# First batch of a two-stage attention and ReGLU kernel: idle matmuls at the start, a changed stage order, a changed split of casts

## Chip, cores and metric

The kernel runs on one core of a Trainium2 chip. The metric is device time in microseconds (us), the median of several executions. Before the change: 700.3 us, median of 5 runs from 699.91 to 702.34 (702.34, 700.5, 700.3, 700.12, 699.91).

## What is computed

Inputs in float32: `x` (4 batches, 12416 rows, 128 columns), 32 `inducing` rows of 128, and three feed-forward weights. Cut to what matters:

```python
h   = softmax(scale * I @ x.T) @ x        # per batch: 32 rows h, over all 12416 rows of x
a   = softmax(scale * x @ h.T) @ h        # per batch: every row of x against those 32
out = (relu(a @ w_gate) * (a @ w_val)) @ w_out      # 128 -> 1536 -> 128
```

Nothing of a batch's second line can start before its `h` is complete, since `h` sums over all rows of that batch.

## The kernel before

**Two kinds of work.** For each batch a first phase computes `h`; after it a long loop computes attention and feed-forward for the rows, 512 at a time and in pairs. The first phase of batches 1 to 3 is spread through the loop of the batch ahead of it. The first phase of batch 0 has nothing to hide behind: the loop can't start before it has ended. The change is in that phase alone.

**First phase of batch 0.** The 97 tiles of 128 rows come in 16 parts (`sizes`, lines 73 to 77): nine of 8 tiles (j0, j1, j2, j4 to j9), six of 4 (j10 to j15), and as j3 a single tile. SP (SyncE) issues their loads in this order, then those of the weights (L251 to L253). No edit touches a load. Each part passes through four stages, each of which issues on fixed engines:

- `cast` (L271): float32 to fp16 into `x16`. The first `h` tiles go to POOL (GpSimd, L278), the others to ACT (ScalarE, L280). For 8 tiles the split is 4 and 4, for 4 tiles 2 and 2. The single tile goes to DVE (VectorE, L275).
- `turn` (L264): PE (TensorE) transposes the part tile by tile into a PSUM bank (L268); DVE copies the result to `xT` (L269).
- `score` (L282): PE multiplies each tile with the inducing rows (L287); ACT takes the exponential into `p1` (L289).
- `sums` (L291): PE adds up the softmax denominators (L297 for the large parts, L306 for the small) and the 32 rows `hT_ps` (L309).

In addition `reduce` (L311) folds the large parts' denominators on DVE, L295 adds them in on PE, and `idle` (L260) issues matmuls of 512 columns whose results nobody reads. The PSUM tiles of `turn` and `score` take turns in three banks of tag "g"; `p1` has four buffers.

**The order.** The engines run what they are given in program order. That order is written by a small planner (lines 319 to 339): each stage of each part gets a due time, computed from the number of tiles landed and a few constants, and the stages are emitted in order of due time. From the part that begins at tile 64 (`late`, j9) on, 1.4 is added, and there three idle matmuls precede the turn. A due time isn't a wait; it only decides which stage is ahead of which in each engine's queue.

**After it** (lines 340 to 354): POOL casts the weights (L341), three idle matmuls, `finish_h` (DVE, L145 and L147), then the first matmuls with `h` (L178 and L159), DVE's copy `hgv` (L349), and the loop (L924 on), where ACT's relu (L998) and DVE's product (L1010) are the main work.

Of the kernel before, what the change touches and what calls it, by code (L numbers as in the profile page):

```python
# [11 lines left out]
FP16 = mybir.dt.float16  # L12
# [6 lines left out]
def kernel(  # L19
# [16 lines left out]
    nc = tc.nc  # L36
# [3 lines left out]
    P = 128  # L40
    assert C == P and M == 32 and N % P == 0 and DFF % P == 0
    NT = N // P
    BLK = 512
# [15 lines left out]
    def bank(tag, name, shape=None, dtype=FP32):  # L59
        return psum.tile(  # L60
            shape or [P, BLK], dtype, tag=tag, bufs={"g": 3, "v": 2, "o": 1}[tag], name=name
        )

    def st(shape, dtype, tag, bufs, name=None):
        return sb.tile(shape, dtype, tag=tag, bufs=bufs, name=name or tag)
# [32 lines left out]
    eye16 = constp.tile([P, P], FP16, name="eye16")  # L98
# [8 lines left out]
    nc.vector.memset(ones16, 1.0)  # L107
    minus1 = constp.tile([P, 4 * TPB], FP32, name="minus1")
    nc.gpsimd.memset(minus1, -1.0)

    ind16 = constp.tile([M, C], FP16, name="ind16")
    nc.vector.tensor_copy(out=ind16, in_=ind32)
# [114 lines left out]
    z1a, idle_ps = z1a_ps[:, 0 : 8 * M], z1a_ps[:, BLK : 2 * BLK]  # L227
# [28 lines left out]
    n_parts = len(parts)  # L256
# [3 lines left out]
    def idle(ps, n, rhs):  # L260
        for _ in range(n):
            nc.tensor.matmul(ps[:, 0 : rhs.shape[-1]], eye16, rhs, start=True, stop=True)
# [8 lines left out]
    def cast(j):  # L271
        t0, t1 = parts[j]
        x32, dst, n = x32s[j], x16[:, t0:t1, :], t1 - t0
        if n == 1:
            nc.vector.tensor_copy(out=dst, in_=x32)  # L275
            return
        h = n // 2 if n != 4 or j == n_parts - 1 else 2
        nc.gpsimd.tensor_copy(out=dst[:, 0:h, :], in_=x32[:, 0:h, :])  # L278
        if h < n:
            nc.scalar.copy(out=dst[:, h:, :], in_=x32[:, h:, :])  # L280
# [38 lines left out]
    stages = []  # L319
    landed = 0  # L320
    late = [j for j in range(n_parts) if parts[j][0] >= 64 and parts[j][1] < NT][0]
    for j, (t0, t1) in enumerate(parts):
        n = t1 - t0
        landed += n
        at = 0.16 * landed + (1.4 if j >= late else 0)
        stages.append((at - (0.6 if j == n_parts - 1 else 0), 0, j, cast))
        at += 0.1 + 0.065 * n
        if j == late:
            idles = lambda j: idle(idle_ps, 3, xT[0][:, 0:4, :].rearrange("p t c -> p (t c)"))
            stages.append((at, 1, j, idles))  # L330
        stages.append((at, 2, j, turn))
        if j == n_parts - 1:
            stages.append((at + 0.3, 3, j, reduce))
        at += 0.05 * n + 0.5 + 0.068 * n + (0.6 if n > 4 else 0.15)
        stages.append((at, 3, j, score))
        at += 0.025 * n + 0.6 + 0.026 * n + (0.6 if n > 4 else 0.3)
        stages.append((at, 4, j, sums))
    for _, _, j, f in sorted(stages, key=lambda e: e[0:3]):
        f(j)
# [160 lines left out]
    def plan_phase1(b):  # L500
# [9 lines left out]
        for q in range(NCH):  # L510
# [17 lines left out]
            at = at0 + 14 * q if q < NQ else at0 + 7  # L528
            post[at + 3].append(load)
            post[at + 11].append(cast)  # L530
            post[at + 15].append(transp)

# [383 lines left out]
    idle_ps = bank("o", "idle_ps")  # L916
# [7 lines left out]
    at = 0  # L924
# [3 lines left out]
    while True:  # L928
# [24 lines left out]
        if jobs:  # L953
            j = jobs[0]
# [89 lines left out]
```

The softmax here doesn't subtract the row's maximum and nothing guards it: scores larger than these inputs give would overflow.

## Time and profile before

| | |
|---|---|
| profiled execution | 700.05 us |
| its span on the core | 698.3 us (1.75 us lie around it) |
| median of 5 runs | 700.3 us |
| busy share of the span, PE / DVE / ACT / POOL | 91% / 97% / 96% / 53% |
| DMA, share of the 16 engines' time taken by the main queue (q1) | 47.9% |
| first product of the loop that lasts (L1010, 1024 columns) | starts at 29.72 us |

How to read it: DVE and ACT are busy for nearly the whole span, but that is an average. Their busy time in the first 25 us is 11.01 and 12.96 us; the loop starts only after that. A row of the timeline has its start, its length, the engine, the line, the operation and how many instructions were merged (x8); a bracket tells how long the engine was idle before it, and who ended that. The chain of waits has start, length, engine, tile and line.

### The profile page before, as it was taken

To read this page: it belongs to the slowest core of one execution; us is meant where nothing else is said; L and a number is where in the kernel's file an instruction comes from. 1 tells how busy PE (TensorE), PEld (TensorE's weight loads), DVE (VectorE), ACT (ScalarE), POOL (GpSimd) and SP (SyncE) were. 2 spreads that over 40 slices of the span, in tenths; PEclk is the share of its full clock that TensorE was granted. 3 is DMA by queue.
4 is the path that set the end of the run, shared out by engine and by line. 5 is a ranking of instruction groups with operands and counts; after the bars stand their busy time and mean duration, and the time that the engine had idled before them with its cause. 6 is when DMAs were issued, how large, how long until landed. Compare 5 with 4: busy or idle time off the path is not lost.

```text
span 698.3 us, 13986 instructions
## 1 busy us (share of the span) xinstructions
PE 632.4 (91%) x4571; PEld 181.3 (26%) x4571; DVE 676.5 (97%) x617; ACT 672.7 (96%) x1381; POOL 370.7 (53%) x680
## 2 busy tenths in 40 slices
PE   6999998999999999999999999998999898888897
PEld 5422222222222222222222222222222222222224
DVE  4699999999999999999999999999999999999997
ACT  4799999999999999999999999999999999999996
POOL 4618647645276565665257474873534543534443
PEclk9999999999999999999999999999999999999999
DMA  9666776541666848513176776533223231231222
GB/s 346 222 127 177 168 171 168 116 84 62 137 174 161 209 135 167 132 58 92 50 193 166 205 185 146 131 95 69 68 72 85 57 92 56 80 85 53 76 56 91
DMA packets 142633, 87.57 MB, mean 125 GB/s; under 512 B 117184, under 2 KB 125664, under 8 KB 140256
## 3 DMA queue, kind: packets, MB, share of 16 engines
q1 hardware_dynamic: 142368, 86.60, 47.9%
q8 instruction: 35, 0.57, 0.3%
q14 instruction: 38, 0.31, 0.2%
q10 hardware_dynamic: 192, 0.08, 0.1%
HBM read 27.80 MB, written 25.43 MB: 76 GB/s over the span
## 4 chain that ended last, share of the span: by engine, by line
ACT 40%; PE 26%; issue 18%; DVE 14%; DMA 2%; SPq 0%; POOL 0%; ACTq 0%; DVEq 0%
ACT g L998 29%; DVE gv L1010 13%; PE o_ps L690 10%; PE v_ps L901 8%; ACT oT L696 6%; PE g_ps L901 3%; ACT p2q L194 2%; ACT p1T L549 1%; PE xT_ps L268 1%; PE o_ps L757 1%; DMA gv<-in_x_dram 1%; ACT hgv L169 1%; DMA out_dram<-osb 1%; DVE xT L269 0%; DMA o<-oT 0%
## 5 line engine op out<-in xcount | busy, mean ns | idle before, releaser
L1010 DVE TENSOR_TENSOR gv<-g,v_ps 128x1024 f16<-128x1024 f16 (+1 forms) x578 | 657.2, 1209 | 3.4 <-ACT g L998 1.0
L998 ACT ACTIVATE g<-g_ps 128x512 f16<-128x512 f32 (+1 forms) x1168 | 603.5, 618 | 6.6 <-PE g_ps L901 1.9
L690 PE MATMUL o_ps<-gv,wo 128*128 128x512 f16 x1128 | 352.4, 384 | 46.0 <-ACT oT L696 45.8
L707 POOL TENSOR_SCALAR osb<-o,z2i 128x128 f32<-128x128 f16 x380 | 164.5, 447 | 229.9 <-DMA o<-oT 219.0
L901 PE MATMUL g_ps<-p,hgv 32*128 32x512 f16 x1152 | 282.5, 379 | 0.8 <-ACT g L998 0.5
L901 PE MATMUL v_ps<-p,hgv 32*128 32x512 f16 x1152 | 223.6, 384 | 5.5 <-DVE gv L1010 4.3
L901 PEld LDWEIGHTS <-hgv 32*128 32x128 f16 x2400 | 66.7, 91 | 267.2 <-issue 262.9
L690 PEld LDWEIGHTS <-wo 128*128 128x128 f16 x1176 | 80.8, 97 | 212.5 <-issue 198.7
L446 POOL TENSOR_TENSOR z2i<-zt,minus 128x16 f32<-128x16 f32 (+3 forms) x31 | 73.2, 2363 | 0.5
L696 ACT CAST oT<-o_ps 128x512 f16<-128x512 f32 (+1 forms) x98 | 59.3, 605 | 0.1
L439 POOL TENSOR_TENSOR zt<-zt 128x32 f32<-128x32 f32 (+5 forms) x124 | 34.9, 281 | 9.7
L517 POOL CAST x<-x 128x2048 f16<-128x2048 f32 x18 | 34.0, 1890 | 11.2 <-DMA x<-in_x_dram 10.7
L439 POOL TENSOR_TENSOR zt<-p2T 128x256 f32<-128x256 f16 (+3 forms) x31 | 17.4, 561 | 32.0 <-DMA p2T<-p2q 17.2
L269 DVE COPY xT<-xT_ps 128x1024 f16<-128x1024 f16 (+1 forms) x15 | 8.6, 583 | 9.4 <-PE xT_ps L268 8.7
L593 POOL TENSOR_TENSOR zq<-p1g 128x256 f32<-128x256 f16 x18 | 12.0, 668 | 6.9 <-DMA p1g<-p1T 6.9
L278 POOL CAST x<-gv 128x512 f16<-128x512 f32 (+1 forms) x15 | 7.9, 528 | 11.7 <-DMA gv<-in_x_dram 11.6
L194 ACT ACTIVATE p2q<-s_ps 128x512 f16<-128x512 f32 x22 | 13.4, 611 | 0.0
L268 PE MATMUL xT_ps<-eye,x 128*128 128x128 f16 x97 | 10.4, 258 | 2.2 <-POOL x L278 1.3
L595 POOL TENSOR_TENSOR zq<-zq 128x256 f32<-128x256 f32 x15 | 10.9, 725 | 1.2
L289 ACT ACTIVATE p<-s_ps 128x256 f16<-128x256 f32 (+2 forms) x16 | 5.2, 333 | 6.3 <-PE s_ps L287 6.2
L280 ACT CAST x<-gv 128x512 f16<-128x512 f32 (+1 forms) x15 | 7.5, 532 | 3.8 <-DMA gv<-in_x_dram 3.8
L549 ACT ACTIVATE p1T<-s1T_ps 128x512 f16<-128x512 f32 x18 | 11.0, 612 | 0.0
(93 smaller groups left out, 165.6 us busy)
## 6 DMA issues: line engine op xcount, KB each, us to landing
out_dram<-osb SPq DMA_DIRECT2D x95, 256.0 KB, 2.2
x<-in_x_dram SPq DMA_DIRECT2D x18, 1024.0 KB, 5.7
p<-p2q SPq DMA_DIRECT2D x88, 64.0 KB, 2.0
gv<-in_x_dram SPq DMA_DIRECT2D x9, 512.0 KB, 6.7
o<-oT SPq DMA_TRANSPOSE x98, 2.4
gv<-in_x_dram SPq DMA_DIRECT2D x6, 256.0 KB, 8.5
x<-in_moe_w_out_dram SPq DMA_DIRECT2D x1, 768.0 KB, 9.6
x<-in_moe_w_gate_dram SPq DMA_DIRECT2D x1, 512.0 KB, 7.1
```

What stands on the lines that cost most here:

```text
L194: nc.scalar.activation(out=p2q, in_=ps, func=AF.Exp, scale=sm_scale)
L268: nc.tensor.transpose(ps[:, t - t0, :], x16[:, t, :], eye16)
L439: nc.gpsimd.tensor_tensor(out=dst, in0=v[:, :, :, 0:m], in1=v[:, :, :, m : 2 * m], op=ALU.add)
L446: nc.gpsimd.tensor_tensor(out=z2i, in0=v[:, :, :, 0], in1=minus1[:, 0 : n * g].rearrange("p (n g) -> p n g", n=n), op=ALU.pow,)
L517: nc.gpsimd.tensor_copy(out=s["x16"][:, t0:t1, :], in_=s["x32", q])
L549: nc.scalar.activation(out=p1T, in_=ps, func=AF.Exp, scale=sm_scale)
L690: nc.tensor.matmul(c["ps"][:, 0:w], wo[:, i, :], gv(i), start=(i == 0), stop=(i == NFF - 1))
L696: nc.scalar.copy(out=oT[:, 0:w], in_=c["ps"][:, 0:w])
L707: nc.gpsimd.tensor_scalar(out=osb[:, t, :], in0=o16[:, t, :], scalar1=zz, scalar2=zz, op0=ALU.mult, op1=ALU.mult,)
L901: nc.tensor.matmul(ps[:, cols], hgv[:, s * P : (s + 1) * P], p2, start=True, stop=True)
L998: nc.scalar.activation(out=g16[:, k * w : (k + 1) * w], in_=ps[:, 0:w], func=AF.Relu)
L1010: nc.vector.tensor_tensor(out=dst[:, ks, :], in0=g16[:, ks, :], in1=v[:, ks, 0:w], op=ALU.mult)
```

## The change

Four edits. (1) A tile `warm` of zeros is made on POOL, and eight matmuls of 512 columns with it stand first in PE's order; one more stands ahead of the turns of j1 and j2. (2) In the four-tile parts, the last excepted, POOL casts 3 tiles and ACT 1, where it was 2 and 2. (3) The due times of `score` and `sums` have other constants. (4) The last part's `cast` is due 0.3 ahead of its landing, where it was 0.6.

```diff
+    warm = st([P, BLK], FP16, "oT", 4)
+    nc.gpsimd.memset(warm, 0.0)
+    warm_ps = bank("o", "warm_ps")
+    for _ in range(8):
+        nc.tensor.matmul(warm_ps, eye16, warm, start=True, stop=True)
...
-        h = n // 2 if n != 4 or j == n_parts - 1 else 2
+        h = n // 2 if n != 4 or j == n_parts - 1 else 3
...
-        stages.append((at - (0.6 if j == n_parts - 1 else 0), 0, j, cast))
+        stages.append((at - (0.3 if j == n_parts - 1 else 0), 0, j, cast))
...
+        if 0 < j < 3:
+            stages.append((at, 1, j, lambda j: idle(idle_ps, 1, warm)))
         stages.append((at, 2, j, turn))
...
-        at += 0.05 * n + 0.5 + 0.068 * n + (0.6 if n > 4 else 0.15)
+        at += 0.05 * n + 0.5 + 0.068 * n + (0.6 if n != 4 else 0.3)
         stages.append((at, 3, j, score))
-        at += 0.025 * n + 0.6 + 0.026 * n + (0.6 if n > 4 else 0.3)
+        at += 0.025 * n + 0.6 + 0.026 * n + (0.8 + 0.6 if n == 1 else 0.8 if n == 8 else 0.3)
         stages.append((at, 4, j, sums))
```

In the engines' queues this comes to the following. PE: eight idle matmuls ahead of the transpose of the inducing rows, two more later; the score of the single tile j3 moves behind that of j1, its sums behind the turn of j5; the turns of j7 and j8 move ahead of the sums of j4 and j5; small exchanges from j8 on. ACT: the cast of j4 moves ahead of the exponential of j3; five casts are 128 columns wide where they were 256. POOL: one memset ahead of everything that waits for data; five casts are 384 columns wide where they were 256. DVE's and SP's orders stay as they were, and no DMA is added, taken away or moved. The first use of the buffer that `warm` held waits, among other things, for that memset.

## The prediction

> **What bounds the kernel now.** I read three things in this order: the busy time by stage, the chain of waits of the first 36 us, and the timeline there. The stage table (columns: stretch, its length, busy time of PE, weight loads, DVE, ACT, POOL, granted clock, DMA share, GB/s):
>
> ```profile
> 0.00:5.00 5.00, 0.20 (x1) 0.10 (x1) 1.38 (x8) 1.43 (x2) 0.86 (x8) 1.00 0.59 198
> 10.00:15.00 5.00, 4.80 (x89) 4.06 (x86) 2.24 (x4) 3.34 (x8) 2.45 (x4) 1.00 1.03 406
> 30.00:35.00 5.00, 4.89 (x33) 1.67 (x33) 5.00 (x5) 5.00 (x12) 4.08 (x5) 1.00 0.42 174
> ```
>
> From 30 us on ACT and DVE are full; nothing in the change touches that loop. Before it, PE and DMA are full and ACT is not. So the change is worth what it moves the loop's start, and the loop carries that to the end if nothing in it hangs on a fixed time. The chain says what the start hangs on:
>
> ```profile
> 12.86 0.05 issue
> 12.91 0.61 PE xT_ps L268 x4
> 13.52 0.21 PE s_ps L287 x8
> 13.73 0.21 PE z1a_ps L297
> 13.94 0.21 PE hT_ps L309 x8
> 14.15 0.56 PE xT_ps L268 x8
> 14.71 0.19 PE s_ps L287 x8
> 14.91 0.12 PE z1a_ps L297
> ...
> 24.58 0.10 PE hT_ps L309 x4
> 24.68 0.66 PE z1a_ps L262 x3
> 25.34 0.03 issue
> 25.36 0.40 PE s_ps L178 x4
> ```
>
> PE almost without a break. The same sum over 256 columns (L297) costs 0.21 at 13.73 and 0.12 at 14.91: PE's rate nearly doubles at about 14.1, though the granted clock reads 1.00 in every stage. The timeline agrees:
>
> ```profile
> 6.79 1.04 PE L268 MATMUL xT_ps<-eye,x 128*128 128x128 f16 x8 [0.20 <-POOL x L278]
> 15.06 0.61 PE L268 MATMUL xT_ps<-eye,x 128*128 128x128 f16 x8
> 15.35 1.10 POOL L278 CAST x<-gv 128x512 f16<-128x512 f32 x2 [0.66 <-DMA gv<-in_x_dram]
> 17.94 0.81 PE L262 MATMUL z1a_ps<-xT,eye 128*128 128x512 f16 x3
> 18.16 1.53 ACT L280 CAST x<-gv 128x512 f16<-128x512 f32 x4
> 20.55 0.40 POOL L278 CAST x<-gv 128x256 f16<-128x256 f32 x1 [0.27 <-DMA gv<-in_x_dram]
> ```
>
> Part j9 has landed at 15.35, when POOL casts its half, but ACT casts the other half at 18.16, 2.8 later: ACT's queue has the exponential of j8 ahead of it, and that waits for PE. The last part lands at 20.55.
>
> **Rates.** From the chain, for a part of 8 tiles at the fast rate: transposes 0.46, scores 0.21, sums 0.12 + 0.19 = 0.31; together 0.98. At the slow rate: transposes 0.86 (8 x 0.107; 1.04 less some 0.18 of tail that the merged row at 15.06 also has), scores 0.21, sums 0.42; together 1.49. Parts land every 1.28 (POOL's casts at 10.24, 11.52, 12.79, 14.08). So a slow PE falls 0.2 behind on each part and a fast one gains 0.3. Other steps: DVE starts 0.2 after the last transpose, occupies 0.61 and can be read 0.74 after its start (16.67 to 17.41); an exponential starts 0.46 after the first score (17.42 to 17.88), frees ACT after 0.28 and can be read after 0.4; an ACT cast of 512 columns occupies 0.52, the next transposes go 0.67 after its start.
>
> **The idle matmuls at the start.** POOL's memset of 512 fp16 columns has no row; it lies between its memset of 128 columns (0.20) and its cast of 512 (0.61). I take 0.6, since nothing on POOL waits until 4.89; it ends by 1.95. Eight slow matmuls of 512 columns: three fast ones take 0.66 in the chain at 24.68, so 0.22 each, slow 1.9 times that, 0.42; 8 x 0.42 = 3.4, to about 5.4. Queued behind them is the transpose of the inducing rows, which ran at 4.29; its copy is then there at 5.85 and first needed by the scores of j0 at 7.5. The turn of j0 waits for its cast until 5.55 anyway; it loses at most 0.1, which the wait for the landing of j1 (6.1) covers.
>
> **When PE becomes fast.** No row shows it for the new order. In the trace the rate rose at 14.1: that is 3.7 after PE's work became gapless (10.44), or 8.55 after it became regular (5.55). Put on a start at 1.9 this gives 5.6 and 10.45; the far bound is no gain, 14.1 as now. I take 7.4, towards the nearer bound, since PE then has work without a break from 1.9 to 7.8. [...]
>
> **The walk.** With release at 7.4, and the new queues: turn of j2 ends 9.38, scores of j1 follow, their exponential runs at 9.84, the cast of j4 at 10.12 (10.44 before). From here each part goes: cast on ACT, transposes, sums, scores, exponential. Scores of j4 begin 12.68, of j5 13.64, of j6 14.61, of j7 15.57 (trace of before: 13.31, 14.55, 15.51, 16.47); the cast of j8 is at 14.38, 0.3 behind its landing, where it was 1.2 behind. The turn of j8 ends 15.27, DVE's copy starts 15.47, scores 16.21, exponential 16.67; ACT is free for j9 at 16.95, not 18.16. That is 1.2. The same walk through the old order with release at 14.1 puts this cast at 18.07 and the end of the sums at 24.6, where the trace has 18.16 and 24.68, so I trust it to about 0.1.
>
> **The tail.** From the cast of j9 to the last sum took 24.68 - 18.16 = 6.52. The 3:1 split makes five ACT casts 128 columns wide: 512 take 0.61 and 256 take 0.40, so 128 take about 0.29 and ACT is freed 0.11 sooner each. POOL's become 0.50, inside the 0.66 between landings. DVE's copies of j9 to j11 stand in a row and eat the first three of these; about 0.1 is left: 6.4. The sums then end at 16.95 + 6.4 = 23.35, 1.33 sooner. By the walk against itself (24.6) it is 1.27. At a release of 5.6 the walk ends at 23.3, at 10.45 at 24.1. The new due times alone are worth 0.03 in it, the split 0.15, the release 1.1. The two later idle matmuls (0.22 each at the fast rate, 0.42 slow) lie where PE waits for j2 and the single tile. What is late next is DMA: the last part lands at 20.55 and its ACT cast comes at 20.6.
>
> **The loop.** `hgv` needs the first halves of the weights, cast by 22.50, at 24.3; the second halves, cast by 25.88, at 26.9. The third weight is cast at 28.46 and needed ten slots into the loop. POOL's row sums (L439, 28.97) can't come before that cast, so they end some 0.3 later against the loop; SP's next transposes behind them wait in the trace already and feed work 20 slots later. I cost all this at nothing; without that slack it takes back up to the whole 1.3. The memset's wait on the shared buffer is tens of us old. Sum: 698.3 - 1.3 = 697.0 of span, plus 1.75 around it: **698.8**. The profiled execution lies 0.25 below the median of the runs, so against 700.3 this is 1.5 less, -0.21%. For the spread: a release between 5.6 and 10.45 gives 698.6 to 699.5.
>
> **Rivals.** (A) *No earlier release*: idle matmuls on zeros don't count, or the rate rises only with the dense work. Then the walk of the new order at 14.1 ends at 24.6: **700.0**. For it: PE's bursts from 5.55 to 8.9 didn't raise the rate in the trace. Against it: those had gaps up to 0.75, these have none for 5.9. (B) *The loop gives it back*: the start moves but the weights or SP's queue hold the loop: 699.4 to 700.0, **699.7**. For it: the margins of 1.0 and 1.8 above shrink if a weight lands later. Against it: the loop has waits of only a few tenths on ACT and DVE after 30 us. (C) *The rate is lost again*, and it is slower: at the fast rate PE waits 0.3 of each 1.28 for data from 8 to 16, where the old one had no gap from 10.44 to 17.4. If the fast rate needs gapless work, PE drops back. With the slow rate to the end the walk of the new order ends at 28.6, 4 later: **704.0**; with a fresh release at 16 at 25.3, 700.7. It decides from a release after 14.1 on. Against it: three idle matmuls still take 0.81 at 24.53, after seven us with gaps. [...]
>
> **Numbers.** Forecast 0.75, A 0.10, B 0.10, C 0.05. About 0.2% (1.4 us) is what a measurement of this kernel tells from no change; the line against the median is 698.9. The forecast lies on it: of its 0.75 I put 0.54 below and 0.21 above. A and B are within it, C gives slower 0.03 and the rest within. Faster 0.54, within 0.43, slower 0.03. The lower end of the range comes from the last part: landed at 20.55, it needs 0.4 for its cast, 0.25 + 0.2 for its turn, 0.47 on DVE, 0.36 + 0.3 for score and exponential and 0.2 of sums, so the sums can't end before 22.75, 1.9 sooner than now, 698.1. With A at the upper end and 0.1 to 0.15 for the spread of medians: 698.0 to 700.2.
>
> **What would show it.** Right: eight idle matmuls from 1.6 to 2.0 on at 0.42 each, L297 at its fast time by the sums of j0 or j1, the cast of j9 on ACT near 17.0, the last sum near 23.4, L178 near 24.1, and L1010's row of 1.22 at 28.4. Wrong: L297 slow until 14; transposes of eight back above 1.0 between 8 and 16; a wait of L159, L998 or L1010 on POOL or DMA after 24; a loop of another length from its first product to the end.

## The result and the profile after

| | before | after |
|---|---|---|
| median | 700.28 us (74 runs, 699.45 to 702.34) | 698.88 us (40 runs, 698.62 to 699.74) |
| profiled execution / its span | 700.05 / 698.3 us | 698.85 / 697.1 us |
| `h` goes into PE (first matmul of `s_ps<-xT,hT`) | 25.36 | 24.20 |
| first product of the loop that lasts (`gv`, 1024 columns) | 29.72 | 28.56 |
| from there to the end of the span | 668.54 | 668.51 |

The ratio of the runs is 0.998 with a 95% interval of 0.9975 to 0.9984: a gain of 0.2%, on the line that the prediction drew. The start of the loop moved by 1.16, and the loop carried it unchanged to the end (span 1.2 shorter).

Lines of the changed kernel stand 7 further down than before (9 from the planner's end on): L275 is the transpose, L285 and L287 the casts, L304 the sum over 256 columns. The table by stage, columns as before:

```profile
0.00:5.00 5.00, 3.06 (x8) 1.04 (x8) 1.44 (x7) 1.35 (x2) 1.25 (x9) 1.00 0.62 202
10.00:15.00 5.00, 4.28 (x97) 3.80 (x97) 2.79 (x5) 4.05 (x10) 2.46 (x4) 1.00 1.03 405
30.00:35.00 5.00, 4.81 (x36) 1.69 (x34) 5.00 (x5) 5.00 (x11) 3.92 (x4) 1.00 0.24 100
```

PE now works from the first stage on, and from 10 to 15 it has breaks (4.28 of 5 where it had 4.80) although it gets more done (97 matmuls for 89). The loop's stage is as full as it was. The chain of waits of the first 36 us:

```profile
7.88 10.13 DMA gv<-in_x_dram
18.01 0.05 issue
18.06 0.52 POOL x L285
...
23.41 0.10 PE hT_ps L316 x4
23.51 0.66 PE z1a_ps L269 x3
24.17 0.03 issue
24.20 0.40 PE s_ps L185 x4
```

Where PE stood before, from 12 to 18, there is now a landing. PE is last in the chain only after that, from the turns of the four-tile parts to the last sum at 23.51 (24.68 before). The timeline has the reason:

```profile
1.95 3.59 PE L116 MATMUL warm_ps<-oT,eye 128*128 128x512 f16 x8 [1.95 <-DVE stackI L101]
5.63 0.62 PE L275 MATMUL xT_ps<-eye,x 128*128 128x128 f16 x8
6.88 0.62 PE L275 MATMUL xT_ps<-eye,x 128*128 128x128 f16 x8 [0.41 <-POOL x L285]
14.11 0.61 POOL L285 CAST x<-gv 128x512 f16<-128x512 f32 x1 [0.66 <-DMA gv<-in_x_dram]
16.86 1.70 POOL L285 CAST x<-gv 128x512 f16<-128x512 f32 x3 [2.14 <-DMA gv<-in_x_dram]
16.93 0.81 ACT L287 CAST x<-gv 128x512 f16<-128x512 f32 x2
```

The idle matmuls run at 1.95, and the very first transposes of eight take 0.62 instead of 1.03. The trace's record of the granted clock begins at 5.40 here and at 14.26 before; in front of its first record the clock column simply reads 1.00, so the slow stretch must be read off the matmul rows. ACT casts j9 at 16.93 instead of 18.16. It is no longer ACT's queue that is late: j9 itself landed at 16.83, 1.5 later than before, when j8 had landed on time at 14.1.

### The profile page after: what moved, and what is told of

Its sections match the earlier page's. It is cut to its first block, busy times and chain, and to the rows that moved or that the text cites. A ratio compares the mean times of both kernels' runs of the same rounds, so it can differ in the third digit from the quotient of the medians.

```text
span 697.1 us, 14008 instructions
## 1 busy us (share of the span) xinstructions
PE 634.1 (91%) x4581; PEld 180.6 (26%) x4581; DVE 676.7 (97%) x617; ACT 672.4 (96%) x1381; POOL 373.1 (54%) x681
## 4 chain that ended last, share of the span: by engine, by line
ACT 40%; PE 24%; issue 19%; DVE 13%; DMA 2%; SPq 0%; ACTq 0%; POOL 0%; DVEq 0%
ACT g L1007 30%; DVE gv L1019 13%; PE o_ps L699 10%; PE v_ps L910 8%; ACT oT L705 6%; PE g_ps L910 3%; DMA gv<-in_x_dram 2%; ACT p2q L201 2%; ACT p1T L558 2%; PE o_ps L766 1%; ACT hgv L176 1%; PE h_ps L624 0%; PE idle_ps L269 0%; ACT p L196 0%; DVE gvr L1019 0%
## 5 line engine op out<-in xcount | busy, mean ns | idle before, releaser
L285 POOL CAST x<-gv 128x512 f16<-128x512 f32 (+2 forms) x15 | 8.4, 566 | 10.9 <-DMA gv<-in_x_dram 10.8
L287 ACT CAST x<-gv 128x512 f16<-128x512 f32 (+2 forms) x15 | 7.2, 495 | 4.5 <-DMA gv<-in_x_dram 4.5
L185 PE MATMUL s_ps<-xT,hT 128*32 128x512 f16 x108 | 10.8, 389 | 0.1
L275 PE MATMUL xT_ps<-eye,x 128*128 128x128 f16 x97 | 8.3, 220 | 2.3 <-DVE x L282 0.7
```

## The experiments

Times are medians, ratios are against the kernel before in the same series, with their 95% intervals. "Last sum" is the end of PE's sums, 0.06 after DVE starts on the denominators (24.62 and 24.68 before); "loop" is the start of the first 1024-column product. The expectations put clock records and instruction packets 0.24 later than the timeline's zero does; in the text they are counted from that zero.

**Which edit makes the gain.** The idle matmuls alone, on the old order and the old split:

```diff
+    warm = st([P, BLK], FP16, "oT", 4)
+    nc.gpsimd.memset(warm, 0.0)
+    warm_ps = bank("o", "warm_ps")
+    for _ in range(8):
+        nc.tensor.matmul(warm_ps, eye16, warm, start=True, stop=True)
```

> The kernel before with nothing but the zero tile and the eight idle matmuls at the start: old due times, old 2:2 split, no later idle matmuls. Theory (the early clock release is the gain): PE at the fast rate by 6, the last sum at 23.5 to 23.7 against 24.68 before and 23.51 after, so 698.9 to 699.1. Rival (the new order and split make the gain, the idle matmuls only go with them): the last sum near 24.5, 699.8 to 700.3.

Measured: 698.96, ratio 0.9987 (0.9978 to 0.9996), last sum 23.57, loop at 28.61. The theory holds: this edit alone comes within 0.1 of the changed kernel's time and its median is 1.05 below that of the kernel before in its own series (700.01). In its trace the clock record begins at 4.59.

The reverse, the changed kernel with `for _ in range(8)` and the two later idle matmuls taken out:

> The changed kernel without the eight idle matmuls at the start and without the two later ones; new due times and 3:1 split stay. Theory: the rate rises at 14 to 17 as in the kernel before, the last sum at 24.5 to 25.6, so 699.9 to 700.8, no faster than before. Rival (order and split make the gain): 698.9 to 699.2.

Measured: 699.74 against 700.01, ratio 0.9998 (0.9989 to 1.0007), last sum 24.36, loop at 29.41; eight transposes still take 1.03 at 7.05. No difference from before is shown. The trace is 0.3 ahead of the first trace of before, so with a late release the order and the split may be worth some tenths; the runs don't settle it.

The split put back (`else 2` for `else 3`):

> The changed kernel with the old 2:2 split of the four-tile casts. Theory (the split is worth 0.15): last sum at 23.65 against 23.51, time 698.9 to 699.2. Rival (ACT is no longer the late one at the end, since DMA now ends the waits there): no difference, last sum at 23.5.

Measured: 698.97, ratio 0.9985 (0.9976 to 0.9994), loop at 28.59. And the four old constants put back in the due times:

> The changed kernel with the old constants in the due times (all four of them); idle matmuls and 3:1 split stay. Theory (the order is worth 0.03): last sum at 23.45 to 23.65, time within 0.15 of the changed kernel. Rival (the order had to be rewritten for the fast clock): last sum 23.8 or later, 699.2 or more.

Measured: 698.93, ratio 0.9982 (0.9974 to 0.9991), loop at 28.65. Both are within 0.1 of the changed kernel, which is inside the noise. The order needed no rewriting, and the 0.15 for the split was too much.

Without the two later idle matmuls:

```diff
-        if 0 < j < 3:
-            stages.append((at, 1, j, lambda j: idle(idle_ps, 1, warm)))
```

> The changed kernel without the two idle matmuls ahead of the turns of j1 and j2; the eight at the start stay. Theory: they lie in PE's waits and the rate is already high, so the last sum stays at 23.4 to 23.6 and the time at 698.7 to 699.0. Rival (they hold the rate over PE's gaps between 6 and 9): transposes of eight go back above 1.0 us for some microseconds and the time is 699.3 or more.

Measured: 698.98, ratio 0.9984 (0.9975 to 0.9992). The trace is 0.35 behind (loop at 28.91, j9 landed at 17.1 in it), the runs are not. The rate holds without these two matmuls: eight transposes take 0.62 at 7.01 and nine take 0.68 at 8.55.

**How much work it takes.** Four and six in place of eight:

```diff
-    for _ in range(8):
+    for _ in range(4):
```

> The changed kernel with four idle matmuls at the start in place of eight: PE has work from 1.95 to about 3.7, then a gap until the data at 5.5. Theory (it takes some 3.5 us of work with no gap): no release by 5.6; the rate rises somewhere between 8 and 14, the last sum at 23.5 to 24.6, 698.9 to 700.0, and the release time read from the rows says which. Rival (any early work will do): as with eight, 698.7 to 699.0, transposes of j0 at 0.62.

> The changed kernel with six idle matmuls at the start in place of eight: PE has work from 1.95 to 4.5 and a gap until 5.5. With eight the rate rose between 4.8 and 7.75 in seven traces, with four at 13.2. Theory (a stretch without a gap of about 3.5 us is needed): no release before 8, time 699.6 to 700.2 as with four. Rival (the amount of early work counts, small gaps do no harm): release by 8 in this trace, 698.8 to 699.2.

Measured: four 699.89, ratio 0.9997 (0.9988 to 1.0006); six 699.98, ratio 0.9993 (0.9984 to 1.0002). With either no gain is shown in the median. The timeline of the kernel with six:

```profile
1.94 2.74 PE L116 MATMUL warm_ps<-oT,eye 128*128 128x512 f16 x6 [1.94 <-DVE stackI L101]
5.55 1.04 PE L275 MATMUL xT_ps<-eye,x 128*128 128x128 f16 x8 [0.73 <-POOL x L285]
6.82 1.05 PE L275 MATMUL xT_ps<-eye,x 128*128 128x128 f16 x8
14.50 0.72 PE L275 MATMUL xT_ps<-eye,x 128*128 128x128 f16 x8
```

PE is busy to 4.8 (the last 0.2 is the transpose of the inducing rows) and idles 0.73 before j0 at 5.55. In this trace the rate rises only at 14.77, as late as in the kernel before (with four: at 12.96). In the changed kernel PE has work from 1.95 to 7.7 with no gap above 0.41. In all nine traces with eight, sixteen or as much idle time in smaller pieces the clock record begins between 4.59 and 7.53. So a little too little is worth nothing that the medians show.

What the clock records show of it: the full rate lasts 682.67 us from the release on before the change, 692.91 after it, and 6.83 in the trace with 128 tiny matmuls further down, ahead of a slow stretch of 3.41. That is 200, 203, 2 and 1 times 3.413. In the 3.41 us ahead of the release PE is busy for 3.2 us or more in thirteen of the fourteen traces (3.21 before, 3.41 after), and for 2.65 in the one with the eight alone (1.18 to 4.59). With six, PE is busy for 2.88 of the 3.41 us from 1.94 on, and the rate didn't rise. So PE's busy time over such a stretch doesn't tell the six from the eight; what does isn't shown.

Sixteen:

> The changed kernel with sixteen idle matmuls at the start in place of eight. Theory: the first eight take 3.5 us at the slow rate and the other eight some 1.8 at the fast one, so PE is busy until 7.3 to 7.5; the turns of j0 and j1 wait for that (5.6 and 6.9 now), and DVE and ACT behind them; the last sum at 24.1 to 24.4, 699.4 to 699.8. Rival (the first parts have enough slack, since later landings end the waits): no difference, 698.7 to 699.0.

Measured: 700.07, ratio 0.9998 (0.9989 to 1.0007), last sum 24.54, loop at 29.58. Idle matmuls that outlast the wait for data take the gain back:

```profile
1.94 5.72 PE L116 MATMUL warm_ps<-oT,eye 128*128 128x512 f16 x16 [1.94 <-DVE stackI L101]
7.71 0.62 PE L275 MATMUL xT_ps<-eye,x 128*128 128x128 f16 x8
```

The turn of j0 begins 2.1 later than in the changed kernel, and 1.0 of it reaches the loop. The expectation was 0.3 too low in the runs, 0.14 in the trace.

**Why j9 lands late.** The table of DMA queues has an instruction queue (packets, MB, share of the 16 engines' time), here before the change:

```profile
q8 instruction: 35, 0.57, 0.3%
```

That is 16 KB a packet, and for PE's 4571 matmuls and 4571 weight loads one packet per 261. The first packet inside the span comes at 16.47 before and at 14.66 after, and takes 1.05 and 1.11 us. The first late landing is j13 before, the third due after the packet's start, and j9 after, the first due after it. To move it, the same idle time cut into more instructions:

```diff
-    for _ in range(8):
-        nc.tensor.matmul(warm_ps, eye16, warm, start=True, stop=True)
+    for _ in range(32):
+        nc.tensor.matmul(warm_ps[:, 0:P], eye16, warm[:, 0:P], start=True, stop=True)
```

> The changed kernel with 32 idle matmuls of 128 columns at the start in place of 8 of 512: the same 3.4 us of slow PE work, but 48 more PE instructions ahead of everything else. In the two traces the first 16 KB packet of the instruction queue comes at 16.71 before and at 14.90 after, and the landing that comes 1.1 to 1.5 late is that of j13 before and of j9 after. Theory (PE's instruction fetch delays one DMA engine and with it every later part): the packet comes 2 to 4 us sooner, at 11 to 13, and the late landing is that of j7 or j8; the last part still lands near 20.7 and the last sum stays at 23.4 to 23.7. Rival (the late landing has nothing to do with the fetch): it stays at j9.

Measured: 699.05, ratio 0.9982 (0.9973 to 0.9991). The packet came at 13.67 only, j8 landed on time at 14.0, and j9 was late again, at 16.56. The theory's place was missed, and the run doesn't tell theory and rival apart. A stronger edit is 128 of 32 columns, `warm_ps[:, 0:M]` and `warm[:, 0:M]`, in place of 8 of 512: 240 more PE instructions (120 matmuls and 120 weight loads) ahead of everything else.

> [...] Theory (the fetch of PE's instructions delays one DMA engine and with it all later parts): the first packet comes at 6 to 10 us instead of 14.9, the first late landing is that of j2 to j5, and a second packet near 15 delays a later part again; the last part lands at 21.2 or later (20.76 now) and the last sum 0.3 to 1.0 later, 699.1 to 699.9. Rival (the late landing has another cause): j9 alone is late, the last part lands near 20.7, 698.7 to 699.1.

Measured: 700.62, ratio 1.0004 (0.9995 to 1.0013), runs from 699.78 to 701.88. The packet came at 7.55, and the landings of j2, j4 and j5, by POOL's casts:

```profile
7.46 0.62 POOL L285 CAST x<-gv 128x512 f16<-128x512 f32 x1 [0.73 <-DMA gv<-in_x_dram]
10.37 0.62 POOL L285 CAST x<-gv 128x512 f16<-128x512 f32 x1 [2.29 <-DMA gv<-in_x_dram]
11.65 0.62 POOL L285 CAST x<-gv 128x512 f16<-128x512 f32 x1 [0.67 <-DMA gv<-in_x_dram]
```

j4 is now the late one, at 10.37 instead of 8.99, and all that follow keep the delay. So the late landing goes with the place of the packet in time (7.55 here, 14.66 in the changed kernel), which the edit moved without touching a load. The second half of the expectation was wrong: a second packet at 16.62 added nothing, and the last part landed at 20.79, as in the changed kernel (20.76). In the two traces of before it was 20.55 and 20.37. The packet's place goes with which part is late, and less with when the last one comes (20.2 to 21.1 in the fourteen traces).

In this trace the kernel was slow for another reason, the prediction's third rival. The table by stage:

```profile
6.20:9.50 3.30, 2.34 (x45) 1.78 (x43) 1.98 (x5) 1.46 (x4) 1.15 (x2) 1.00 1.04 411
9.50:13.00 3.50, 1.93 (x40) 1.55 (x38) 1.14 (x2) 2.04 (x6) 1.30 (x3) 0.96 1.03 411
13.00:16.30 3.30, 3.30 (x56) 3.17 (x55) 1.59 (x3) 2.39 (x5) 1.78 (x3) 0.52 1.03 394
16.40:20.00 3.60, 3.60 (x81) 3.13 (x78) 1.33 (x3) 2.25 (x7) 2.65 (x5) 1.00 1.06 384
```

and of its timeline:

```profile
11.04 0.62 PE L275 MATMUL xT_ps<-eye,x 128*128 128x128 f16 x8 [1.29 <-POOL x L285]
13.98 1.01 PE L275 MATMUL xT_ps<-eye,x 128*128 128x128 f16 x8
16.51 0.61 PE L275 MATMUL xT_ps<-eye,x 128*128 128x128 f16 x8
```

PE waited 1.29 for the late part and was busy for only 1.93 of the second stretch's 3.5; in the third the granted clock was 0.52, in the fourth 1.00 again. The last sum came at 25.08, the loop at 30.12, later than before the change. That is the profiled execution. The other ten runs have a mean granted clock of 0.999 or 1.000, where 3.4 us at half rate would leave 0.998 or less, and yet they took 699.78 to 701.88. The loss of the rate doesn't explain those; what does stays open.

**Before once more:**

> The kernel before once more, for a second trace of it. Theory (its rate rises only with its first gapless stretch, at a moment that differs from run to run): the rise lies between 13 and 17, and the last sum follows it by the walk: 24.4 at 13, 25.0 at 15, 25.6 at 17. Rival (the rise is tied to a fixed place in the order of work): at the same sums as in the first trace, those of j4, near 14.1.

Measured: one run of 700.62; the clock record begins at 14.24 (14.26), at the same turn as in the first trace, last sum 24.71 (24.68), loop at 29.76 (29.72). Two traces can't tell theory and rival apart. They do show that the spread of the old kernel's runs isn't all from the first phase: this run was 0.57 longer than the first, and 0.54 of it came after the loop's start (669.08 against 668.54). From what, stays open.

**What ends the phase now.** In the changed kernel PE runs without a break from 20.28 to the last sum. Part of that is the fold of the denominators, a float32 matmul of 0.35:

```diff
-    z1s = st([P, M], FP32, "z1s", 1)
+    z1s = st([P, M], FP16, "z1s", 1)
...
-            nc.tensor.matmul(z1, ones32[0:1, :], z1s[0:1, :], start=False, stop=False)
+            nc.tensor.matmul(z1, ones16[0:1, :], z1s[0:1, :], start=False, stop=False)
```

This kernel keeps those denominators in fp16 for the fold, a change in the computation.

> The changed kernel with z1s in fp16 in place of float32, so that the matmul that adds the large parts' denominators to the others is one fast pass: 0.35 in the chain now, 0.03 then. In the trace of the changed kernel PE runs without a gap from 20.28 to the last sum. Theory (PE's work is what ends the phase now): last sum at 23.2 to 23.3 against 23.5, 698.5 to 698.7. Rival (the last landing and its way through cast, copy and exponential end it): no difference, 698.8 to 699.0.

Measured: 698.84 in 8 runs, ratio 0.9976 (0.9966 to 0.9986), last sum 23.42, loop at 28.47. The trace is 0.09 ahead, the median 0.04: not to be told from the changed kernel. The fold became 0.18 in place of 0.34 from its start to the next sums, and it still waits for DVE's reduction, which ends at 22.59. No version here is shown to beat the changed kernel.

## Why the prediction was right, point by point

- **The gain sits in the start of the loop, and the loop passes it on.** Right. From the loop's first product to the end it took 668.5 in eleven of thirteen other traces and in this one, whatever the first phase did; the two others, 669.03 (128 idle matmuls) and 669.08 (before again), have no explanation here. The second rival, a loop that gives it back, didn't happen.
- **Release.** Taken at 7.4, found at 5.4 in this trace and between 4.6 and 7.5 in all nine with eight or as much: earlier than the near bound of 5.6 in two of them. The miss of 2 us cost next to nothing, since by the prediction's own walk a release at 5.6 instead of 7.4 moves the last sum by 0.05. The far bound of 10.45 was too wide, and nothing came in between: in the other five, with none, four or six, the release is as late as before (13.0 to 14.8). What sets the moment isn't shown: the nine releases lie within 2.9 us of one another, and the earliest, at 4.59 in the trace with the eight alone, has PE busy for only 2.65 of the 3.41 us before it. In the trace with 128 tiny matmuls the rate was lost 6.83 us after the release and came back 3.41 us later.
- **The walk.** The scores of j4 to j7 were due at 12.68, 13.64, 14.61 and 15.57 and came at 12.34, 13.29, 14.29 and 15.55; the exponential of j8 at 16.65 for 16.67, the cast of j9 at 16.93 for 16.95. The last agreement is partly luck: ACT was free at 16.93, but j9 had landed at 16.83 only.
- **A step that failed: landings as before.** The prediction kept the old landing times and named only the last part as late next. The edit moved the first instruction packet from 16.47 to 14.66, and with it the late landing from j13 to j9. It cost little: kernels in which j9 landed near 15.5 and j10 came late instead (the idle matmuls alone, the 2:2 split) start the loop at 28.61 and 28.59, this one at 28.56.
- **Mis-sized: the tail and the split.** 6.4 from the cast of j9 to the last sum, measured 6.58; 0.15 for the 3:1 split, measured 0.09 in the medians, inside the noise. The last sum came at 23.51, not 23.35, and the gain of the span was 1.2, not 1.3.
- **The rival that is slower** was told with the right mechanism but with a wrong condition: the rate wasn't lost with breaks of 0.7. In the one trace that lost it, the one with 128 tiny matmuls, the break was 1.29, and PE was busy for 1.96 of the 3.42 us before. Transposes run at the higher rate too: eight of them went from 1.03 to 0.62, and the rate held from 4.59 to 8.01 in the trace with the eight alone, where they are 1.24 of PE's 2.09 busy us. What they do for the rate by themselves no run shows.
- **Faster by over 0.2% at 0.54, within at 0.43**: the measured ratio is 0.998, with both sides in its interval.

## What to carry to other kernels

When a kernel's first microseconds are a wait for data and PE's rate matters after them, try idle matmuls up to the first data, without a gap and not beyond: here eight alone gave 1.05 us, and six or sixteen nothing that could be shown. Look for a slow PE in the matmul rows and not in the clock column (here 1.03 against 0.62 for eight transposes, with the column at 1.00 for both), and compare PE's work per part with the time between landings: here a slow PE needed 1.49 for each 1.28, so its rate reached the end. Count the instructions too: here 120 more idle matmuls, with as many weight loads, brought the instruction queue's first packet from 14.66 to 7.55 and moved the late landing from j9 to j4, though no edit touched a load.

## What the runs showed of the hardware

- The clock was lost again once: in the trace with 128 tiny matmuls PE was busy for 1.96 of the 3.42 us before 12.73 (one gap of 1.29) and then ran 3.41 us at 0.50. With 2.09 busy of 3.42 (4.59 to 8.01 in the trace with the eight alone, longest gap 0.64) it stayed.
- Matmuls on zeros were enough for the release: with the eight alone it came at 4.59, before the first transpose (5.06).
- The first instruction packet took 1.05 us in its DMA queue before and 1.11 after. In thirteen of the fourteen traces one load landed 0.7 to 1.5 late, and all later ones kept the delay; where the packet's start is given above (16.47, 14.66, 13.67, 7.55) it was one of the first three due after it. In the one with four idle matmuls, where it came at 17.53, only the last part was late, by 0.4.
